# Another order of a batch pipeline's steps and other engines for its copies out of PSUM, in a fused attention and token-mixing kernel

## Chip, cores, metric

One core of one Trainium2 chip. The metric is the time of one execution in microseconds on the device; the runs of one kernel are listed with their median. A run counts as slow when it lies more than 1.5% above the fastest of the same kernel.

## The reference

Eight batches, each on its own. An attention of 8 heads (576 positions, 64 wide) has two parts: a coarse one on means of four neighbours, and a local one in which a position sees three neighbours on each side. Their sum goes through a token mixer.

```python
q_d, k_d, v_d = (mean over groups of 4 positions of q, k, v)
out_up    = repeat(softmax(q_d k_d^T / 8) v_d, 4)
out_local = softmax(where(|i - j| < 4, q k^T / 8, -1e9)) v
x  = (out_up + out_local) as (B, 576, 512)
W  = (x w_q) (x w_k)^T / 8
y  = relu(W x) w_out
```

Inputs and output are float32.

## The kernel before

A batch is cut into some fifty steps, and one table, `ORDER`, says in which order the steps of several batches are laid down; `(-2, "vd")` is step `vd` of the batch two behind the current one. Within an engine, instructions run in the order in which they were laid down. The engines are PE (TensorE: matmuls, their results land in PSUM; PEld in the views is its weight loads), ACT (ScalarE), DVE (VectorE) and GpSimd (POOL in the views). The granted clock, PEclk, is the share of its full clock that PE got. The steps that matter here:

```python
def ps(dtype=FP32, name="ps"):    # two banks wide; three of these take turns
    return ps2.tile([128, 2, 512 ...], dtype, name=name, tag=slot("ps", 3))
def psm(dtype=FP32, name="psm"):  # one bank; two take turns
    ...
ENG = {... "vd0": "a", "xT0": "d", "xT1": "a", "M2": "d", "M2b": "d", "og1": "a", ...}
# which engine does a copy: a = ACT, d = DVE, p = GpSimd; "name@3" is for batch 3 alone

def vd():          # coarse values
    pv = ps(name="pv")
    ...            # 16 matmuls into pv
    evac(b, "vd0", vd0..., pv[:, :, 0:260])                       # ACT reads pv
    dve.tensor_tensor(vblk, pv[... 260 ...], blk, op=ALU.mult)    # DVE reads pv
def cs(i): ...     # coarse scores: matmuls into pcs, ACT takes exp into Ec
def ca(i): ...     # coarse output: matmuls into pca from Ec, vd0 and vblk; DVE divides
def av(i): ...     # local output: matmuls into pav; DVE: reciprocal rz, then x = pav * rz
def xt(i):         # i = 0: 8 transposes of x into px (both banks)
    for j in range(2):
        evac(b, "xT%d" % j, xT[j], px[bank j])                    # DVE, then ACT
def wt(): ...      # matmuls into pw; DVE adds wTd into wT;   wkt transposes wT
def m2():          # 7 matmuls into pm2
    evac(b, "M2", M2[0:64], p_[0:64]); evac(b, "M2b", M2[64:128], p_[0:64])
def mx(r): ...     # matmuls into pmx; relu into rmx
def og(i): ...     # 8 matmuls into po; copy into os; store

ORDER = [... (-3, "xt0"), (-3, "wtd"), (-2, "score2"), (-2, "av0"), (-2, "cs1"), ...
         (-2, "av1"), ... (-6, "og1"), ... (-3, "wt"), ... (-4, "mx1"), ... (-2, "vd"), (-3, "wkt"),
         ... (-2, "av4"), ... (-2, "ca0"), (-2, "ca1"), ...]     # [cut]
for i in range(-8, B + 8):
    for lag, name in ORDER: ...steps[i + lag][name]()
```

A full iteration uses 24 of the two-bank tiles. As 24 is a multiple of three, a step has the same buffer in every iteration, and it needs the one that was used three two-bank tiles earlier to have been read. A tile that two engines read is read by one after the other: the second waits for the first (in the trace ACT waited 3.9 us in all for DVE's `xT`, and DVE 4.2 us for ACT's vd), although the halves of `px` lie in different banks and `vblk` needs nothing that `vd0` writes. The Trainium skill, "PSUM — Partial Sum Buffer", Specifications (TRN2), says that ScalarE and VectorE can access PSUM in parallel as long as no bank collides. This program does not use that: ACT's copy of px started 0.02 us after DVE's copy of the other bank had ended.

The softmax here doesn't subtract the row's maximum and nothing guards it: scores larger than these inputs give would overflow.

## Time and profile before

| | before |
|---|---|
| median (first three runs) | 190.47 us (189.70 to 191.61) |
| profiled span | 187.8 us |
| busy: PE, ACT, DVE, GpSimd | 148.3, 118.2, 113.0, 109.4 us |
| PE (TensorE) idle before its last matmul | about 35 us, 24 of it before the first `m2` |

I cut the execution at the first matmul of each batch's `m2` step, which I read from PE's timeline. The table of stretches gives, for each cut, its length and the busy time of each engine. Rows are: stretch, length, then busy us of PE, PEld, DVE, ACT, GpSimd (instructions in brackets), granted clock, DMA share, GB/s. The kernel before, rows 1, 4, 5 and 9 of nine:

```profile
core 0: us, PE busy (x) PEld busy (x) DVE busy (x) ACT busy (x) POOL busy (x), PEclk, DMA share, GB/s
0.00:59.70 59.70, 35.31 (x834) 29.31 (x835) 35.48 (x92) 33.65 (x39) 44.09 (x71) 0.89 1.01 305
...
89.98:108.79 18.81, 17.27 (x348) 11.74 (x344) 12.06 (x27) 13.12 (x20) 16.10 (x16) 1.00 1.11 260
108.79:126.71 17.92, 16.32 (x343) 11.22 (x340) 11.35 (x26) 13.21 (x20) 12.57 (x12) 1.00 0.75 180
...
169.43:187.80 18.37, 12.80 (x79) 5.28 (x75) 3.58 (x5) 8.81 (x12) 0.00 (x0) 0.92 0.50 186
```

A full period lasts 18.81 us with the extra `ol` step (it comes every second batch) and 17.92 without. PE has 1.5 to 1.6 us of idle time in each; every other engine has more (GpSimd, the next, is busy 16.10 of 18.81 us in the first). Where the idle time sits, the chain of waits shows (start, us, what); one period of it:

```profile
111.86 0.89 PE px L27 x8
112.78 0.65 DVE xT L27
113.45 0.56 ACT xT L27
114.05 0.34 PE pcs L27 x8
...
118.67 0.65 ACT rmx L27
119.33 0.49 ACT vd L27
119.84 0.71 DVE vblk L27
120.59 1.11 PE pca L27 x20
```

Twice per period the chain leaves PE for two copies that follow each other: px by DVE, then by ACT, before `pcs` may write that buffer; and pv by ACT (behind ACT's `rmx`), then by DVE, before `pca`. In total PE waited 3.6 us for `xT` at `pcs` and 5.2 us for `vblk` at `pca`.

At the start there is something else. PE's timeline (start, us, engine, line, operation, tiles; in brackets the idle time before):

```profile
39.61 0.38 PE L27 MATMUL pu<-id,vT 64*64 64x64 f16 x22
44.45 0.79 PE L27 MATMUL pu<-id,vT 64*64 64x64 f16 x42 [4.46 <-issue]
45.17 1.97 PE L27 MATMUL pq<-id,q 128*128 128x128 f32 x8
```

In the middle of 64 equal transposes PE stops for 4.46 us and waits for nothing that the profile shows; the eight q transposes after it take 1.97 us, where a later batch needs 1.02 to 1.09. The granted clock was 0.50 from 45 to 47 us.

### The profile page before, as it was taken

Reading aid. Unit: us, or ns where it says so; the run is one execution under the profiler, and the core shown is the slowest. Engines: PE = TensorE matmul, PEld = TensorE weight load, DVE = VectorE, ACT = ScalarE, POOL = GpSimd, SP = SyncE. Lnnn points to the kernel's source line nnn. Section 1 sums busy time; section 2 is a strip of 40 time slices with the busy share of each in tenths; the row PEclk is TensorE's granted clock in tenths of the full one; section 3 lists DMA queues with packets and bytes.
Section 4 is the critical chain, followed back from the end, with each engine's and each line's share of the span. In section 5 each row is a group of like instructions: output and inputs, shape, how many; then the busy total and the mean of one; then the engine's idle time right before and its main releaser. Section 6 shows DMA issues by size and latency. Waiting matters only on the chain.

```text
span 187.8 us, 6701 instructions
## 1 busy us (share of the span) xinstructions
PE 148.3 (79%) x2906; PEld 102.5 (55%) x2906; DVE 113.0 (60%) x256; ACT 118.2 (63%) x164; POOL 109.4 (58%) x132
## 2 busy tenths in 40 slices
PE   0451858855889879879988998799889889999890
PEld 0341646745766766656755675666556655554330
DVE  6229985441487787785765576647576848834110
ACT  1446688652648767895975597578836782445742
POOL 7889965990089989979949953990592000000000
PEclk9999995795899999999999999999999999999996
DMA  5999999999999929999999999818543011343555
GB/s 220 387 411 387 410 407 236 369 152 222 248 273 228 186 57 269 198 203 222 302 206 232 285 345 144 215 45 196 114 167 113 8 65 50 115 156 123 197 197 223
DMA packets 42989, 40.31 MB, mean 215 GB/s; under 512 B 32656, under 2 KB 33232, under 8 KB 42960
## 3 DMA queue, kind: packets, MB, share of 16 engines
q1 hardware_dynamic: 42880, 39.85, 77.4%
q8 instruction: 23, 0.38, 0.9%
q14 instruction: 6, 0.05, 0.1%
q10 hardware_dynamic: 80, 0.03, 0.1%
HBM read 30.41 MB, written 9.44 MB: 212 GB/s over the span
## 4 chain that ended last, share of the span: by engine, by line
PE 66%; ACT 11%; POOL 8%; issue 7%; DVE 6%; POOLq 0%; ACTq 0%
PE po L27 15%; PE pm L27 7%; PE px L27 5%; PE pca L27 5%; PE psc L27 5%; PE pk L27 4%; PE pq L27 4%; PE pcs L27 4%; PE pw L27 3%; POOL Pq L27 3%; DVE vblk L27 3%; PE pmx L27 3%; DVE xT L27 2%; ACT vd L27 2%; POOL k L27 2%
## 5 line engine op out<-in xcount | busy, mean ns | idle before, releaser
L27 POOL TENSOR_TENSOR sk<-kT 128x1152 f32<-128x1152 f16 x7 | 14.7, 2106 | 30.1 <-DVE rz L27 26.3
L27 PE MATMUL po<-wo,rmx 128*128 128x512 f16 x128 | 30.1, 379 | 0.0
L27 DVE TENSOR_TENSOR x<-pav,rz 128x512 f16<-128x512 f32 x40 | 27.7, 692 | 1.4
L27 ACT COPY os<-po 128x1024 f32<-128x1024 f32 x16 | 16.2, 1012 | 16.9 <-issue 7.6
L27 POOL CAST q<-q 128x1152 f16<-128x1152 f32 x14 | 21.9, 1574 | 0.0
L27 POOL CAST k<-k 128x1152 f16<-128x1152 f32 x14 | 21.8, 1577 | 0.1
L27 PEld LDWEIGHTS <-rmx 128*128 128x128 f16 x144 | 13.3, 98 | 14.0 <-issue 0.2
L27 ACT ACTIVATE E<-psc 128x928 f16<-128x928 f32 (+1 forms) x24 | 19.7, 822 | 1.2 <-PE psc L27 0.8
L27 PE MATMUL pk<-id,k 128*128 128x128 f32 x64 | 10.6, 320 | 12.3 <-ACT k L27 7.5
L27 ACT ACTIVATE rmx<-pmx 128x576 f16<-128x576 f32 x24 | 14.9, 650 | 8.2 <-PE pmx L27 8.2
L27 ACT COPY kT<-pk 128x1024 f32<-128x1024 f32 x8 | 8.1, 1016 | 16.9 <-PE pk L27 16.9
L27 DVE RECIPROCAL rz<-pav 128x8 f32<-128x8 f32 x40 | 8.2, 205 | 15.1 <-PE pav L27 14.5
L27 ACT ACTIVATE Ec<-pcs 128x672 f16<-128x672 f32 (+1 forms) x16 | 14.0, 878 | 3.5 <-PE pcs L27 3.5
L27 PEld LDWEIGHTS pk<-id,k 128*128 128x128 f32 x64 | 8.6, 167 | 12.7 <-POOL Pm L27 7.4
L27 POOL TENSOR_TENSOR sq<-qT 128x1152 f32<-128x1152 f16 x7 | 14.8, 2107 | 0.0
L27 PE MATMUL pav<-v,E 64*64 64x65 f16 x640 | 13.6, 196 | 1.2 <-ACT v L27 0.7
L27 DVE TENSOR_TENSOR wT<-pw,wTd 128x576 f16<-128x576 f32 x8 | 6.1, 758 | 11.3 <-ACT os L27 8.3
L27 PE MATMUL px<-id,x 128*128 128x128 f32 x80 | 12.7, 293 | 0.0
L27 DVE TENSOR_SCALAR M<-pm 64x512 f16<-64x512 f32 x16 | 10.9, 683 | 2.9 <-PE pm L27 2.3
L27 PE MATMUL pca<-vblk,Ec 128*128 128x260 f16 x32 | 8.5, 288 | 5.2 <-DVE vblk L27 5.2
L27 PEld LDWEIGHTS <-E 64*64 64x64 f16 x640 | 11.1, 110 | 2.4 <-issue 1.7
L27 DVE COPY xT<-px 128x464 f32<-128x464 f32 (+1 forms) x15 | 7.9, 529 | 7.5 <-PE px L27 4.9
(97 smaller groups left out, 340.5 us busy)
## 6 DMA issues: line engine op xcount, KB each, us to landing
k<-in_k_dram SPq DMA_DIRECT2D x16, 576.0 KB, 8.4
q<-in_q_dram SPq DMA_DIRECT2D x16, 576.0 KB, 8.0
out_dram<-os SPq DMA_DIRECT2D x16, 512.0 KB, 2.8
v<-in_v_dram SPq DMA_DIRECT2D x60, 128.0 KB, 6.1
v<-in_v_dram SPq DMA_DIRECT2D x4, 576.0 KB, 10.2
wo<-in_moe_w_out_dram SPq DMA_DIRECT2D x2, 512.0 KB, 11.7
out_dram<-ol SPq DMA_DIRECT2D x4, 256.0 KB, 2.1
w<-in_moe_w_q_dram SPq DMA_DIRECT2D x1, 128.0 KB, 9.0
```

Of the source, the lines that this page charges most:

```text
L27: return lambda *a, **k: self._tc.keep_in_program_order(f_(*a, **k))
```

## The change

Its intent, as given: the steps of the batches in another order and other engines for the copies out of PSUM, so that two engines never follow each other on one PSUM tile in a chain. There are two parts, a new `ENG` table and new `FIRST`/`ORDER` tables; no step is added or removed. The core of the diff, with lines re-wrapped to show what moves:

```diff
 ENG:
-  "cq1": "p", "u1": "d", "u2": "d", "cv1": "p", "cv2": "a", "kT": "a", "rq": "d", "rk": "d",
-  "xT0": "d", "wTd": "a", "wd": "a", "M2": "d", "M2b": "d",
+  "cq1": "d", "u1": "a", "u2": "a", "cv1": "a", "cv2": "p", "kT": "d", "rq": "a", "rk": "a",
+  "xT0": "a", "wTd": "d", "wd": "d", "M2": "a", "M2b": "a",
   [cut: the entries for batch 0 alone]
 FIRST:
-  load k0 k1 q0 q1 of batch 0, k0 k1 of batch 1, v0 v1 of batch 0, ...
+  load q0 k0 k1 q1 v0 v1 of batch 0, k0 k1 of batch 1, ...
 ORDER (whole; loads and casts of weights cut):
-  m2(-4) uv0 cv1 cv0(-2) mx3 mx2(-5) tq(-1) xt0 wtd(-3) score2 av0 cs1(-2) xt1(-3) uv1(-2) ck1(0) tr(-1)
-  cs0 av1 cv2(-2) sk1(-1) og1(-6) cq0(0) wt(-3) sq1(-1) cq1(0) ol(-5) sq2(-1) mx1(-4) sk2(-1) vd(-2)
-  wkt(-3) vn0(-1) av4(-2) vn1(-1) ca0 ca1(-2) tk(0) og0(-5) score1 tv(-1) av3(-2) ck0(1) wks(-3) odt(-2)
-  score0(-1) av2(-2) mx0(-4)
+  cs0(-3) ck1(-1) sk1(-2) wtd xt1(-4) cs1(-3) score1(-2) cq1(-1) sk2(-2) og1(-6) av0(-3) wt(-4) score2 sq2(-2)
+  ca1(-3) ol(-6) cv0 uv1(-2) wkt(-4) score0(-2) ca0(-3) uv0(-2) tk vn0(-1) mx1(-5) vn1 tq(-1) wks(-4)
+  mx0 mx2(-5) odt(-3) cv1(-2) tr(-1) cv2(-2) ck0(0) av1 av4(-3) mx3(-5) m2(-4) av3(-2) cq0(0) vd(-2) xt0(-3)
+  og0(-5) tv(-1) av2(-2) sq1(-1)
```

(The number in brackets is the lag of the steps named before it.) In the new order `vd` comes one entry of lag, about half a period in time, ahead of its `ca`, `og0`, `av2` and, in two of the batches, `tv` stand between `xt0` and the next `cs0`, and `tk`, `tq` and `tr` of a batch come in one iteration. pv is still read by ACT and then by DVE.

## The prediction

> **What bounds the kernel now.** From 56 us on, TensorE (PE). The chain of waits is 66% PE, and the table of stretches between successive transposes of k (56.06, 70.44, 85.03, 103.83, 121.71, 140.5 us) shows PE busy 12.29 of 14.38, 12.96 of 14.59, 17.26 of 18.80, 16.28 of 17.88 and 17.31 of 18.79 us; ACT (13.1 in the full ones) and DVE (11.4 to 12.1) have room. The 1.5 us of PE idle per period sit at two places of the chain: (a) px is copied by DVE (0.65), only then by ACT (0.56), and pcs, which needs the buffer, waits about 0.65. (b) pv is read by ACT (0.49), only then by DVE (vblk, 0.71), and pca waits about 0.75.
> Before 56 us PE is busy only 32 us: GpSimd builds constants until 14.06, then casts batch 1's k, whose transposes stand before batch 0's scores (started at 18.05 and 20). From 39.99 to 44.45 PE stops, "issue", inside a run of small transposes. The gaps at 27.5, 36.0 and 40.0 lie about 244 PE instructions apart while DMA is full: I read them as instruction fetch (the Trainium skill, "Runtime: NRT & Kernel Launch", Instruction fetch mechanics: blocks of 256 instructions over a DMA queue). After it the q transposes take 1.97 us instead of 1.09, which agrees with "TensorE: Matmul & The Clock Gate", Part 1 (an idle PE falls back to half clock).
>
> **What the change does.** No matmul is added or removed. Both px copies go to ACT; vd moves an iteration ahead of its pca, which hides (b); og0 and av2 stand between px and the next pcs, which hides (a). Per batch ACT loses kT 1.02, wTd 0.29, wd 0.27, cv2 0.61 and gains rq, rk 0.78, xT 0.55, M2 1.2 (estimate), cv1 1.04: +1.4, to about 14.4. DVE loses xT 0.64, M2 1.37, rq, rk 0.77 and gains kT 1.2 (estimate), cq1 0.85, wTd, wd 0.58: even. GpSimd loses 2.6, gains 0.5. All stay below PE's 16.3 to 17.3; walking one period by hand with three buffers, PE waits for almost nothing.
> Start: batch 0's scores come near 15.5 instead of 20 us, but DVE's early queue (two sums of 2.56, qd, u1) keeps batch 0's coarse scores near 28. By the third k transposes (34 us in both) the new order has done some 4 us more PE work. The pipeline is about an iteration shorter.
>
> **Time.** About 1 us in each of seven periods (7), start and fill 3 to 5, and 0 to 5 from the fetch gap, which may come back; ACT at 85% gives back some. 190.5 - 12.5 = **178 us**, range 170 to 187. Faster by over 2% 0.87, within 2% 0.09, slower 0.04.
>
> **What would show it.** Right: no DVE-then-ACT px pair and no vd-vblk-pca triple in the middle of the chain; full periods near 17 us at 95% PE busy; pcs and pca waits (5.6, 5.2 us in total) near zero; GpSimd busy 15 us less, ACT 10 more; last matmul near 171. Wrong: PE still 92% busy in full periods, waiting for ACT copies (M2, os, xT).
>
> **What would make it wrong.** "Issue" gaps of several us in the DMA-full first 50 us; ACT becoming the limiter; DVE's early queue holding batch 0; a longer drain (four mx copies, og and the last output in a row).

## The result

| | before | after |
|---|---|---|
| runs, us | 191.61, 189.70, 190.47, 189.18 | 178.89, 180.41 (slow), 176.67, 179.19 |
| median | 190.08 | 179.04 |
| busy: PE, ACT, DVE, GpSimd | 148.3, 118.2, 113.0, 109.4 | 147.0, 126.7, 110.5, 97.5 |
| first `m2` starts | 59.70 | 53.54 |
| PE idle, before / between first and last / after last `m2` | 24.4 / 9.5 / 5.6 | 20.6 / 3.6 / 5.7 |
| profiled span | 187.8 | 176.8 |

The ratio is 0.937, with a 95% interval of 0.925 to 0.949. Ratios here are the mean time of one kernel's fast runs over that of the other's fast runs of the same rounds, so not quite the ratio of the medians.

The changed kernel's stretches, rows 1, 4, 5 and 9:

```profile
core 0: us, PE busy (x) PEld busy (x) DVE busy (x) ACT busy (x) POOL busy (x), PEclk, DMA share, GB/s
0.00:53.54 53.54, 32.97 (x864) 27.77 (x865) 36.65 (x92) 36.39 (x46) 44.43 (x76) 0.97 1.01 318
...
85.43:103.07 17.64, 17.52 (x348) 11.56 (x344) 12.50 (x26) 14.15 (x22) 11.73 (x11) 1.00 0.93 234
103.07:120.29 17.22, 16.87 (x344) 11.43 (x340) 11.57 (x25) 14.03 (x22) 11.88 (x11) 1.00 0.97 289
...
160.42:176.80 16.38, 10.73 (x63) 4.43 (x59) 2.05 (x3) 8.03 (x11) 0.00 (x0) 0.98 0.41 157
```

The full periods went from 18.81 and 17.92 us to 17.64 and 17.22, and PE is idle for 0.12 and 0.35 us in them instead of 1.54 and 1.60. One period of its chain of waits:

```profile
87.37 0.41 PE pv L27 x16
87.78 1.02 PE px L27 x8
88.80 1.74 PE po L27 x8
90.62 1.01 ACT os L27
91.63 0.92 ACT Ec L27
92.59 1.89 PE po L27 x8
```

After px PE goes straight on with `po`; in this period neither the px copies nor vd and vblk are in the chain. (In the next one a single px copy by ACT is, for 0.46 us, before ACT's copy of `po`; no copy by DVE stands before it.) What is left is ACT: the copy of `po`, then the exponential of `pcs` behind it, and only then may the next `po` use the buffer of `pcs`. It costs little: PE has other matmuls meanwhile and is idle for 0.12 us in the whole period. The gaps of PE at the start are there too, but shorter:

```profile
30.63 0.22 PE L27 MATMUL pav<-v,E 64*64 64x65 f16 x3 [1.27 <-issue]
...
34.91 0.45 PE L27 MATMUL pu<-id,vT 64*64 64x64 f16 x33 [1.17 <-issue]
```

The 11.0 us between the two spans are, by subtraction of the stretches: 3.8 us less PE idle before the first `m2`, 6.0 us less between the first and the last, 0.1 us more at the end, and 1.3 us less PE busy time. By length of the stretches the same 11.0 us look different: 6.2 us before the first `m2`, 2.9 between the first and the last (109.7 to 106.9 us) and 2.0 after it. The reason is that PE's busy time fell by 2.3 us before the first `m2` and by 2.1 after the last, and rose by 3.1 between them. The cuts do not part the same work in both orders (834 and 864 matmuls lie before the first `m2`, 79 and 63 after the last), so neither split is exact. Before the first `m2` the mean granted clock also rose from 0.89 to 0.97; what that gave by itself no run separates.

### The profile page after: what moved, and what is told of

Read it like the earlier page. It is cut to its first block, busy times and chain, and to the rows that moved or that the text cites. A ratio compares the mean times of both kernels' runs of the same rounds, so it can differ in the third digit from the quotient of the medians.

```text
span 176.8 us, 6704 instructions
## 1 busy us (share of the span) xinstructions
PE 147.0 (83%) x2906; PEld 99.9 (56%) x2906; DVE 110.5 (63%) x246; ACT 126.7 (72%) x180; POOL 97.5 (55%) x126
## 4 chain that ended last, share of the span: by engine, by line
PE 63%; DVE 11%; DMA 9%; ACT 8%; issue 4%; POOL 2%; SPq 0%; ACTq 0%
PE po L27 16%; PE pm L27 7%; DMA q<-in_q_dram 6%; PE pca L27 5%; PE pav L27 5%; PE pw L27 4%; PE px L27 4%; PE pq L27 4%; ACT Ec L27 4%; PE pk L27 3%; PE pmx L27 3%; DVE od L27 3%; DMA k<-in_k_dram 3%; DVE x L27 2%; ACT os L27 2%
## 5 line engine op out<-in xcount | busy, mean ns | idle before, releaser
L27 DVE RECIPROCAL rz<-pav 128x8 f32<-128x8 f32 x40 | 8.1, 204 | 20.6 <-PE pav L27 20.5
L27 PE MATMUL pk<-id,k 128*128 128x128 f32 x64 | 9.5, 296 | 11.8 <-ACT k L27 9.8
L27 PEld LDWEIGHTS <-E 64*64 64x64 f16 x640 | 9.0, 108 | 11.9 <-issue 10.1
L27 DVE COPY kT<-pk 128x1024 f32<-128x1024 f32 x8 | 9.8, 1223 | 9.0 <-PE pk L27 8.6
L27 PE MATMUL pav<-v,E 64*64 64x65 f16 x640 | 12.5, 197 | 2.7 <-issue 1.3
L27 PEld LDWEIGHTS pk<-id,k 128*128 128x128 f32 x64 | 7.6, 151 | 12.1 <-POOL Pq L27 9.8
L27 POOL CAST q<-q 128x1152 f16<-128x1152 f32 x7 | 11.4, 1630 | 4.8 <-DMA q<-in_q_dram 3.6
L27 ACT ACTIVATE Ec<-pcs 128x1008 f16<-128x1008 f32 (+1 forms) x16 | 13.1, 877 | 1.3 <-PE pcs L27 1.3
L27 POOL TENSOR_TENSOR kd<-sk 128x256 f16<-128x256 f32 (+1 forms) x24 | 13.4, 587 | 0.5
L27 ACT CAST v<-v 128x1024 f16<-128x1024 f32 x12 | 12.5, 1043 | 0.0
L27 PE MATMUL px<-id,x 128*128 128x128 f32 x80 | 11.9, 280 | 0.5 <-DVE rz L27 0.5
L27 ACT ACTIVATE M<-pm 64x512 f16<-64x512 f32 x16 | 9.4, 591 | 3.4 <-PE pm L27 2.9
L27 DVE TENSOR_TENSOR od<-pca,rc 40x512 f16<-40x512 f32 (+1 forms) x16 | 11.0, 687 | 0.6
```

Of the source, the lines that this page charges most:

```text
L27: return lambda *a, **k: self._tc.keep_in_program_order(f_(*a, **k))
```

## The experiments

Theory 1: the order did it. Theory 2: the engines did it, as the intent has it. All kernels gave correct results except the two that are said to be wrong. The columns "full period" are the stretches from the third `m2` to the fourth (with `ol`) and to the fifth (without), of the profiled run; "PE idle" is its sum from the first `m2` to the last. PE's busy time is the union of modelled spans and contains some waiting, so the period is the safer of the two.

| kernel | median us (runs) | ratio to before, 95% interval | full period | PE idle |
|---|---|---|---|---|
| before | 190.08 (4) | 1 | 18.81, 17.92 | 9.5 |
| after | 179.04 (4) | 0.937 (0.925 to 0.949) | 17.64, 17.22 | 3.6 |
| order_only | 192.65 (4) | 1.022 (1.012 to 1.031) | 19.11, 18.72 | 8.9 |
| engines_only | 218.21 (4) | none; its one fast run 214.37 | 26.75, 20.62 | 24.3 |
| before_px_act | 190.73 (4) | none; its one fast run 186.68 | 18.62, 17.79 | 12.1 |
| before_vd_early | 198.20 (4) | none; its one fast run 193.16 | 18.45, 18.43 | 13.3 |
| after_px_split | 180.82 (4) | 0.943 (0.931 to 0.955) | 17.86, 17.34 | 4.4 |
| after_m2_dve | 183.28 (4) | 0.963 (0.954 to 0.972) | 18.56, 18.16 | 8.0 |
| after_three_dve | 185.05 (4) | 0.971 (0.961 to 0.981) | 18.63, 18.19 | 10.0 |
| after_vd_late | 196.08 (4) | none; its one fast run 192.13 | 19.15, 18.67 | 12.6 |
| before_few_loads | 185.83 (1) | none | 18.81, 17.92 | 9.5 |
| after_few_loads | 182.10 (1) | none | 17.63, 17.55 | 3.9 |
| better1 | 180.67 (4) | 0.946 (0.936 to 0.955) | 17.63, 18.47 | 4.7 |
| before_one_engine | 188.11 (6) | 0.987 (0.979 to 0.996) | 18.48, 17.73 | 7.8 |

The kernel before was run beside each group: its medians were 189.31 (7 runs), 190.19 (7), 189.04 (7) and 189.91 (11). The first `m2` of the others is named where it is used. The profiled runs of before_px_act, before_vd_early, after_px_split, after_vd_late and better1 were slow ones; I use their traces to see what waits for what, and compare no times of them closely.

### The two halves of the change: order_only and engines_only

```diff
 order_only:    new FIRST and ORDER, ENG of before
 engines_only:  FIRST and ORDER of before, new ENG
```

> The new order of steps and first loads with the engines of before. Theory 1 (the gain is the order: each copy out of PSUM has other matmuls between it and the matmul that needs its buffer, and the pipeline fills earlier): 178 to 182 us, PE busy 97% or more of a full period although px is again copied by DVE and then by ACT. Theory 2 (the gain is the choice of engines, which ends the successions of two engines on one tile): 186 us or more, with pcs waiting for px copies.

> The order of before with the new engines. Theory 1: 186 to 191 us, since two copies by one engine follow each other just as two copies by two engines do, and the vd-vblk pair is still two engines right before pca. Theory 2: 182 us or less.

Measured: 192.65 and 218.21 us. Both halves alone are slower than the kernel before, and both theories fall. (The time of order_only lies in the range of theory 2, but `pcs` did not wait for a px copy there: the list of waits has none of 0.2 us or more.) The chain of order_only, in one period:

```profile
92.60 0.69 DVE x L27
...
94.13 0.63 DVE M L27
94.78 0.68 DVE M L27
95.50 0.22 DVE rz L27
95.74 0.70 DVE x L27
...
96.49 1.92 PE po L27 x8
```

In the new order several copies for DVE fall due close together: two local outputs, two copies of M2 and another local output. `po` (og0) takes the buffer of that last local output (av3), which DVE reaches only after the rest. The chain of engines_only:

```profile
110.82 2.59 DVE q L27
113.41 0.59 DVE ol L27
114.00 0.62 DVE vblk L27
...
114.66 1.91 PE pca L27 x20
```

Here the cast of q, which the new table gives to DVE, stands in DVE's queue between `wT` and `vblk` in the old order, and `pca` waits for all of it. In that kernel PE was idle 3.3 to 5.1 us in a period, and the mean granted clock of two periods was 0.83 and 0.81; a chain of `po` took 2.98 us there instead of 1.73. The clock did not follow the idle time of a period: with 4.03 us of it another period had 1.00.

From this I formed theory 3: what counts is when the last reader of a buffer is done, and that is decided by what stands ahead of that read in its engine's in-order queue. Where two engines read one tile, the second engine's whole queue stands behind the first's. Order and engines fit together or they don't; a copy has no good engine on its own.

### One wait at a time in the old order: before_px_act, before_vd_early, before_one_engine

```diff
 before_px_act:      -"xT0": "d"   +"xT0": "a"
 before_vd_early:    in ORDER, (-2, "vd") moved from behind mx1 to directly behind (-6, "og1"), ahead of wt
 before_one_engine:  -"xT0": "d", "vd0": "a"   +"xT0": "a", "vd0": "d"
```

> The kernel before, with both copies of px on ACT and nothing else changed. If the two-engine succession on px is what PE waits for: pcs no longer waits 0.65 us a period, about 4 us faster, 186. If the succession is merely serial work of about equal length (ACT twice took 1.00 us in the changed kernel, DVE then ACT 1.30 in this one): at most 0.3 us a period, 188 to 190.5.

The times are inconclusive: three of its four runs were slow ones (up to 193.56) and one was 186.68. The trace, of a slow run, says what became of the wait: `pcs` waits 0.44 us a period instead of 0.57 to 0.63, `pca` as before 0.75 to 0.78, and the two full periods, both at a granted clock of 1.00, are 0.19 and 0.13 us shorter. That is the second expectation: two copies by one engine are serial work of about the same length.

> The kernel before, with only the step vd moved in front of wt (behind og1), so that matmuls of about 2.5 us stand between pv and the pca that needs vblk; still ACT then DVE on pv. Theory 1: the pca wait of 0.7 to 0.8 us a period goes, 3 to 6 us faster, 184.5 to 187.5. Theory 2 (two engines in succession cost by themselves): under 1.5 us.

Measured: 198.20, its one fast run 193.16, a miss. The wait of `pca` did go, but in part it came back somewhere else, as the chain shows:

```profile
104.96 1.85 PE po L27 x8
...
106.89 1.02 ACT os L27
107.90 0.50 ACT vd L27
...
108.42 0.70 DVE vblk L27
109.12 0.68 DVE wT L27
...
109.84 0.29 PE pwk L27 x12
```

ACT copies `os` first, then vd; vblk waits for that, and as DVE works in order, the addition into `wT`, which was due and needs nothing from ACT, waits behind vblk. PE needs `wT` for its next step. DVE waited 13.6 us for ACT's vd in all (before: 4.2 us). This tells why the full periods gained nothing (18.45 and 18.43 us, before 18.81 and 17.92), not where the 8 us went. The profiled run, a slow one, lost its time earlier: rows 2 and 3 of its stretches are 18.20 and 19.81 us (before: 14.02 and 16.26). There `pv`, now earlier, waited 1.15 and 1.21 us for ACT's cast of v, and PE stood still once for 2.82 us, "issue". What the fast run lost, no trace shows. Moving vd also shifts the turn of the three buffers for the steps between its two places, here and in after_vd_late; no run separates that.

> The order of before, with the two successions of two engines that its chain shows undone by engine alone: both px copies on ACT, both reads of pv (vd and vblk) on DVE; nothing else moved. If the succession of two engines on one tile is itself the loss: both waits (0.65 and 0.75 us of PE idle a period) go, 1.5 us in each of seven periods, 179 to 182 us. If the loss is the place in the order (the copies still follow each other on one engine, and the matmul that needs them still comes next): px saves 0.3 us a period, pv saves the 0.5 us for which ACT's rmx stood in front of vd, 184 to 188 us, with some 0.8 to 1.2 us of PE idle left in a full period.

This is the direct test of the intent. Measured: 188.11 us, ratio 0.987. Taking away both successions of two engines, without moving a step, gave 1.3%, a fifth of the change's gain. PE is still idle 1.20 to 1.38 us in a full period, at the same two places, since two copies by one engine follow each other just as well. The direction and the time are as expected for "the place in the order"; the idle time left over is somewhat larger than the 0.8 to 1.2 us that I wrote. At `pcs` the wait shrank from 3.6 to 2.5 us in total; at `pca` it did not (5.2 and 5.3), against the 0.5 us a period that I expected. On DVE, vd no longer stands behind ACT's `rmx`, but behind the addition into `wT` or, every second period, the copy of `ol`:

```profile
116.66 0.76 DVE wT L27
117.42 0.61 DVE vd L27
118.02 0.62 DVE vblk L27
118.69 1.13 PE pca L27 x20
```

### One piece back in the changed kernel: after_px_split, after_m2_dve, after_three_dve, after_vd_late

```diff
 after_px_split:   "xT0": "a" -> "d"
 after_m2_dve:     "M2", "M2b": "a" -> "d"
 after_three_dve:  "xT0", "M2", "M2b", "rq", "rk": "a" -> "d"
 after_vd_late:    in ORDER, (-2, "vd") taken out and (-3, "vd") put in directly ahead of (-3, "ca1")
```

> The changed kernel with the first px copy on DVE again, so that DVE and then ACT follow each other on px. Theory 3 (the engines' in-order queues are coupled by a tile that two of them read: the second engine's whole queue stands behind the first one's, and the loss is what stands behind it): DVE reaches px only after vblk, which stands behind ACT's vd, so ACT's second px copy, the os copy and Ec start about 0.4 us later in each of seven periods, 181 to 184 us. Rival (distance in the order alone hides it, as two other PE steps lie between px and the matmul that needs its buffer): 178 to 180 us.

Measured: 180.82 us; its two fast runs are 178.65 and 179.80. The two times don't tell the two kernels apart (the intervals of 0.937 and 0.943 overlap); the fast runs lie in the rival's range of 178 to 180, so theory 3's 181 to 184 was a miss. Its full periods are 0.1 to 0.2 us longer, in a slow run; no more than that is shown. The succession of DVE and ACT on px costs little where other PE steps stand between.

> The changed kernel with both M2 copies on DVE again (one engine on one tile either way, only 1.2 us of work moved). Theory 3: vblk comes some 0.35 us later but nothing urgent stands behind it, 178.5 to 181 us. If DVE's queue at the end of the iteration is the whole reason why the new order with the old engines was slow: 184 us or more.

Measured: 183.28 us, 4 us above the changed kernel. Theory 3 as I had applied it was wrong about the size: I had looked only at vblk. The chain shows what does stand behind the M2 copies:

```profile
88.30 0.68 DVE M L27
89.00 0.68 DVE M L27
89.72 0.22 DVE rz L27
89.96 0.70 DVE x L27
90.71 1.91 PE po L27 x8
```

It is the buffer of the local output again, which og0 needs. Full periods are 0.92 and 0.94 us longer than in the changed kernel. The new order with the old engines was 1.47 and 1.50 us longer, so this one piece is nearly two thirds of it.

> The changed kernel with px's first copy, both M2 copies and the two remainder copies of q and k on DVE again, all other engines as changed. Theory 3: some 2.8 us of DVE work stand in one run before vblk and px, which the chain of waits of the new order with the old engines showed; 185 to 193 us although ACT has 2.8 us per batch less to do. If ACT's load bounds the changed kernel: faster than 179.

Measured: 185.05 us, at the lower edge of what theory 3 said (its fast runs are 183.42, 184.95 and 185.16). It has almost the same full periods as with M2 alone (0.03 to 0.07 us more); the rest lies in the fill (3.24 us of PE idle in its first stretch between two `m2`, 1.56 with M2 alone). ACT's load does not bound the changed kernel: with 2 us less ACT work per period it is slower.

> The changed kernel with the step vd put back directly in front of the pca matmuls that need vblk, engines unchanged. Theory 3: ACT's os and E copies stand before vd, DVE's vblk behind it, and PE's next step needs vblk, so PE waits 1 to 2 us in each of seven or eight periods, 187 to 195 us. If the place of vd does not matter: 179.

Measured: 196.08 us, most of its runs slow ones, the fast one 192.13. With vd back in front of `pca`, PE waited 11.7 us for vblk, up to 1.5 us at a time:

```profile
87.67 0.59 ACT vd L27
88.29 0.71 DVE vblk L27
...
89.05 0.65 PE pca L27 x10
```

The place of this one step is worth more than the whole gain, as far as one fast run and the trace of a slow one show.

### The loads: before_few_loads, after_few_loads

```diff
 def load(b, nm, u):        # q and k
+    if b >= 2: use the tile of batch b - 2; return
 def load_v(b, n):
+    if b >= 4: use the tile of batch b - 2; return
```

> Wrong results on purpose: the kernel before, in which batches 2 to 7 read the q and k of batches 0 and 1 again, and batches 4 to 7 the v of batches 2 and 3, so that the DMA queues are nearly empty after the first loads; every other instruction stays. If the 4.46 us standstill inside the small transposes is instruction fetch behind a full DMA queue: gone (no issue gap of PE over 1 us after 20 us) and the stretch to the first m2 about 4 to 6 us shorter; full periods unchanged at 17.9 to 18.8 us with 1.5 us of PE idle, as they wait for copies and not for loads. If the standstill is something in the instruction order: still there.

> Wrong results on purpose: the same cut of loads in the changed kernel. If loads matter only at the start: PE's gaps named issue (1.27, 1.17, 0.93, 0.72 us) shrink below 0.5, GpSimd's 20 us of waiting for k loads go, the first m2 comes 2 to 5 us earlier, full periods stay at 17.2 to 17.6 us because PE is 98% busy in them. If the changed kernel is bound by loads in the middle: full periods below 16.8 us.

The times are weak evidence, but the traces are clear about two things. First, full periods are the same as with all loads (18.81 and 17.92; 17.63, and 17.55 against 17.22): neither kernel is bound by loads in the middle. Second, the 4.46 us standstill of the kernel before is gone with the loads. One gap named "issue" of 1.54 us was left at 29.8 us, which my expectation had excluded; the loads that remain were still running then. The first `m2` came 4.0 us earlier (55.75). So the standstill comes and goes with the loads, which is what instruction fetch behind them would do:

```profile
31.30 0.27 PE L27 MATMUL pcs<-qd,kd 64*64 64x168 f16 x4 [1.54 <-issue]
```

The places of these gaps speak for it too. The 14 profiled runs have 40 gaps of PE named "issue" of 0.4 us or more. Count PE's matmuls and weight loads in each trace in the order in which they start: all 40 gaps come after 193 of them plus a multiple of 256 (one after 194), in both orders, whatever PE is doing there; the 4.46 us stand after 962, the 1.54 us after 449. Most places of this kind have no gap. So the rival "something in the instruction order" falls; no run shows the fetch itself.

In the changed kernel, PE had no such gap of 0.4 us or more left, but its first `m2` came later, at 56.05 instead of 53.54. That was not expected. Without the waits for loads GpSimd works on without a pause, and DVE suffers beside it: four weight casts took 3.42 us in the chain, where they took 0.88 us on the timeline of the changed kernel while GpSimd waited; PE's mean clock in that stretch was 0.88 instead of 0.97. The Trainium skill, "Perfetto Trace Analysis", Optimizing Scalar/DVE Operations, says that GpSimd and DVE share an SBUF read port and that a two-port DVE operation holds it as an exclusive lock. This agrees: the cast of q on DVE (128x1152) took 0.82 us at best, and 2.84 us in the changed kernel when a GpSimd addition of 2.12 us ran beside it, about the sum of the two (whether this cast is such an operation, no run shows):

```profile
44.13 2.84 DVE L27 CAST q<-q 128x1152 f16<-128x1152 f32 x1
44.17 2.12 POOL L27 TENSOR_TENSOR sk<-kT 128x1152 f32<-128x1152 f16 x1
```

The two kernels with few loads start equally late (55.75 and 56.05).

### A version meant to beat both: better1

```diff
+ FIRST: k0 k1 q0 q1 of batch 0;  "ck0@0", "cq1@0": "d", "cq1@3": "a", "og0@6": "d"
+ second half of batch 1's k cast right behind its first half
+ in the iteration i = 12 the four mx steps of the last batch ahead of og1
```

> The changed kernel with its start and end mended: batch 0's k loaded first, its first k half and second q half cast by DVE, batch 1's second k half cast before its q half (the chain showed it waiting for q's load), the second q half of batch 3 cast by ACT (DVE took 2.76 us beside GpSimd), the last batch's mx steps ahead of the last but one og1 with one output copy on DVE. 2 to 5 us less idle at the start, about 1 at the end: 174 to 178 us. If the start is bound by the loads of batch 2 rather than by these casts: 178 to 180.

Measured: 180.67 us, ratio 0.946; the two fast runs are 177.76 and 179.92. It is not faster than the changed kernel. (In the profiled run, a slow one, the full period of 18.47 us holds an "issue" gap of 1.22 us.) The start lost 2.3 us of PE idle (18.3 instead of 20.6), but PE's busy time there rose from 33.0 to 37.0 us at a mean clock of 0.91 instead of 0.97, and the first `m2` came at 55.28. The end gained 0.2 us.

## Why the prediction was right

The time (178 predicted, 179.04 measured) and the main mechanism hold: both waits went. How near the number came is in part luck, as the terms of the sum show. Point by point:

- *What bounds the kernel, (a) and (b).* Right. PE's waits at `pcs` for xT (3.6 us before) and at `pca` for vblk (5.2 us) are gone from the list; others of 1.2 us at `pcs` and 1.6 us at `pca` are left.
- *About 1 us in each of seven periods.* Right for the two full periods above, which are 1.17 and 0.70 us shorter (the prediction gave 95% PE busy; it is 98 and 99%). The seven times are not borne out: PE idle between the first and last `m2` fell by 6.0 us, but these seven stretches together are only 2.9 us shorter. The start and the end, 6.2 and 2.0 us shorter, made up for it.
- *vd ahead by an iteration hides (b).* Right, though the distance is half a period and not a whole one (pv at 87.4 us, its `pca` at 96.2 in the period shown). Shown by after_vd_late (11.7 us of waits at `pca`; the turn of the buffers aside). It hides the pair of engines, it does not end it: DVE waited 4.4 us for ACT's vd after the change and 4.2 us before, now off the chain in full periods.
- *og0 and av2 hide (a).* Right as far as it goes (after_px_split). But the prediction gave the order the credit for both waits and counted the engine moves only as load (ACT +1.4 us, DVE "even"). That step of the argument was incomplete. order_only shows that the new order with the old engines is 2% slower than before, and after_m2_dve shows why: in the new order og0 needs the buffer of av3, so whatever stands before av3 in DVE's queue is on the critical path. The engine table has to move the M2 copies away from there.
- *Engine loads.* The estimates held: kT on DVE took 1.22 us (1.2 estimated), an M2 copy on ACT 0.59 (1.2 for two). GpSimd's busy time fell by 11.9 us (15 predicted), ACT's rose by 8.5 (10).
- *Start and shorter fill 3 to 5, fetch gap 0 to 5.* The first `m2` came 6.2 us earlier, within the 3 to 10 of the two terms; the split is not supported. PE idle before it fell by 3.8 us. The gaps named "issue" of more than 0.4 us on PE there add up to 6.3 us before (0.72, 0.69, 4.46, 0.44) and 3.2 after (1.27, 1.17, 0.72), or 4.1 with the 0.93 us that the chain shows behind vblk at 41.46 us, so they account for more than half of it. They lie 256 or 257 matmuls and weight loads apart, or about twice that, and not 244 as the prediction says. Without loads both orders reach the first `m2` at the same time, one look each. I can't show that the order of the first scores bought anything by itself.
- *A longer drain.* It did not come: 5.6 and 5.7 us of PE idle, and the stretch after the last `m2` is 2.0 us shorter, with 63 matmuls instead of 79. The last matmul ended at 172.2 us (171 predicted).

What stays open: which engine moves besides M2, xT0, rq and rk make up the rest of the distance between after_three_dve (185.05) and order_only (192.65); what the higher clock at the start gave; and whether the gaps named "issue" are instruction fetch, for which their places speak.

## What to carry to other kernels

Ask of each PSUM buffer which read ends last, what stands ahead of that read in its engine's in-order queue, and which matmul needs the buffer next; order of steps and choice of engines then have to be set together, since here each half alone lost 2% and 13% (192.65 and, in its one fast run, 214.37 us) and both together won 6%. Two engines reading one tile in succession cost at most 0.1 to 0.2 us a period once the matmul that needs the result came much later (after_px_split, the trace of a slow run); before that, putting both reads on one engine gained 1.3%. When PE is idle in every period, look at the clock as well: in engines_only the granted clock was 0.50 from 114 to 120 us, after a gap of 2.25 us, so that this gap was paid for twice; after one of 2.46 us, at 129.16, it stayed at 1.00.

## What the Trainium skill lacked or had wrong

- "Runtime: NRT & Kernel Launch", Instruction fetch mechanics, calls the cost of crossing a block of 256 instructions mostly hidden. Here PE stood still for 0.72, 0.69 and 4.46 us at places 256 or 257 matmuls and weight loads apart while loads kept the DMA engines busy (a share of 0.92 during the longest); with most loads taken away one gap of 1.54 us was left. If this is fetch, the page lacks that DMA traffic lays it open.
- "TensorE: Matmul & The Clock Gate", Part 1, lets the clock fall to half after an idle window of about 3.4 us. The half clock agrees (0.50 from 45 to 47 us in the kernel before, q transposes of 1.97 us instead of about 1.05). The length does not: in engines_only single gaps of 2.52 and 2.25 us were followed by a granted clock of 0.50 (from 104 to 106 and from 114 to 120 us; eight k transposes took 1.95 us), one of 2.46 us was not.
- None of the pages that I read says that a tile read by two engines puts the second engine's whole queue behind the first's (13.6 us of DVE waiting in before_vd_early, in the trace of a slow run).
